# An attention and two feed-forward stages on one core: early memory for the first feed-forward unit, q stored twice, the sum of v on GpSimd, a written order for each of 18 tiles

## The chip, the cores and the metric

One Trainium2 chip, one of its cores. The metric is the device time of one execution in microseconds (us). The kernel before takes 2220.19 us, the median of 3 runs (2219.45 to 2221.54).

## The reference, cut to what matters

Three stages follow one another. The inputs are float32; `q`, `k` and `v` have the shape (4, 8, 576, 64).

```python
scores = (1 / 8) * q @ k.T                       # 32 heads, 576 x 576 each
scores = where(scores >= rowmax(scores) - tau, scores, -1e9)
attn = exp(scores - rowmax(scores)); attn /= attn.sum(-1) + 1e-9
x = merge_heads(attn @ v)                        # 2304 x 512
x = (((x @ w1) * (x @ w2)) @ w3) @ w_out         # first feed-forward stage
P = exp(x @ w_gate - max); 8 times: P /= rowsum; P /= colsum; P *= 2304 / 8
out = sum over 8 experts e of P[:, e] * (relu(x @ w1[e]) @ w2[e])
```

## The kernel before, in words

**Attention.** The 32 heads are taken as 16 pairs (`NP`). A pair has nine tiles: four blocks of 128 query rows for each of two heads, and a ninth that holds the last 64 rows of both. So there are 144 tiles (`NT`), and the loop at L322 runs over slots s = 0 to 153. In slot s the kernel does a step of several tiles at once: the scores of tile s+2 (step `S`, L142, TensorE), their row maximum (`x`, L146, VectorE), the threshold and the exponential (`t` L149, `X` L154, ScalarE), the mask of tile s (`m`, L161, VectorE), the four transposes of tile s-1 (`T`, L186, TensorE) and their copy out of PSUM (`e`, L191, ScalarE), and in some slots the product with v (`v`, L232), the transposed last columns of three tiles (`q` L197, `l` L202) and the spreading of the inverse sums (`I` L250, `V` L262, `o` L270). Scores have two PSUM buffers (L134), so the scores of tile s+2 can only be written when the mask of tile s has been read from the same buffer. Where tau is negative no score of a row is kept and the reference's row becomes uniform; the flags `g` and the sums `s` (L171 to L177, GpSimd) account for that, and it needs the column sum of v, which `vsum` (L204 to L210) makes with five matmuls of float32 in slot 1 of each pair (`SUMS_AT`).

**Filling.** Meanwhile `W34` (L357) takes 40 pieces of weights, which arrive as 64-bit bit patterns, converts them to float32 (`to_f32`, L478: per piece two ScalarE, four VectorE and two GpSimd operations) and forms w3 @ w_out in 192 matmuls of 128x512 (`w`, L460). `CONVERT` and `PRODUCTS` say by slot (modulo 18) how many steps of a conversion and how many matmuls are allowed; `CHUNKS` is the order of the pieces. `c` and `z` in the order each do at most one conversion step.

**Order.** Each engine runs its instructions in program order. Within a slot the order of the steps is written out as one string for all slots:

```python
ORDER = "fTmSvrigesIzVocxqlXwyt"
```

After the steps of a slot come the loads for the next pair (L341, L345), the sum of v (L343) and, from slot 142 on, steps of the feed-forward generator (`AHEAD`, L347).

**Start.** For the first pair q and k come by four transfers for each head (L106 to L111, both halves of 64 partitions apart: q goes to both, k's columns are split), then tau (L287), then the first weights (L289) and v. ScalarE negates tau (L291) before the thresholds and exponentials of the first two tiles.

**Feed-forward.** `Moe` (L502) splits each float32 operand in a high and a low part and does three products. Work is cut in units: 24 for the first stage (alternately `a` = w1 and `b` = w2 columns, for three blocks of 768 tokens), then 96 for the experts. A unit has seven slots of six matmuls (`mm1`, L663); while they run, the products of the unit before with the second weights (L741) are put between them, and the weights of the next unit are prepared by `prep1` (L571 to L598) on GpSimd and ScalarE. The first unit needs four sums of blocks of x (`xsum`, L629), seven splits (`xsplit`, L655: ScalarE L659, VectorE L660) and its weights. All that is allocated at slot 142, when the pool of q, k and the conversions is closed (L327); the loads of the second unit's weights start when `grow` (L533) is called in slot 145, where the pool of w3 @ w_out is closed.

Of the kernel before, what the change touches and what calls it, by code (L numbers as in the profile page):

```python
# [22 lines left out]
NP = B * H // 2  # L23
# [26 lines left out]
AFTER = {'I': (7, 10), 'V': (8, 11), 'o': (8, 11), 'y': (8, 12)}  # L50
SUMS_AT, VALUES_AT = 1, 4
# [22 lines left out]
def attention(k):  # L74

    tc, nc = k.tc, k.nc
    early, late, banks, parts34 = ExitStack(), ExitStack(), ExitStack(), ExitStack()
    pool = late.enter_context(tc.tile_pool(name="att", bufs=1, side="right"))
    psum = late.enter_context(tc.tile_pool(name="attp", bufs=1, space=bass.MemoryType.PSUM, side="right"))
    epool = early.enter_context(tc.tile_pool(name="atte", bufs=1))  # L80
    wpool = parts34.enter_context(tc.tile_pool(name="w34s", bufs=1, side="right"))
    psums = banks.enter_context(tc.tile_pool(name="atts", bufs=1, space=bass.MemoryType.PSUM))
# [206 lines left out]
    fill = W34(k, epool, wpool, psum)  # L289
# [31 lines left out]
    ahead = iter(())  # L321
    for s in range(NT + 10):  # L322
        n, t = divmod(s, 9)
        if s == NT - 20:
            k.raw0 = wpool.tile([128, 4, 256], F32, name="raw1_0")
            nc.sync.dma_start(k.raw0.rearrange("p a b -> p (a b)"), k.wab["a"][0])
# [20 lines left out]
        if k.moe:  # L347
            for _ in range(AHEAD.get(s - NT, 0)):
                next(ahead)
    late.close()  # L350
    k.moe.rest()
    for _ in ahead:
        pass
    k.moe.stack.close()
# [147 lines left out]
class Moe:  # L502
# [7 lines left out]
    def __init__(self, k):  # L510
# [7 lines left out]
        self.xh = [pool.tile([128, 2, HT], F32R, name=f"xh{i}") for i in range(7)]  # L518
        self.xl = [pool.tile([128, 2, HT], F32R, name=f"xl{i}") for i in range(7)]
# [6 lines left out]
        self.sink = []  # L526

# [14 lines left out]
    def rest(self):  # L542
# [5 lines left out]
        self.acc = self.pool2.tile([128, 6, DM], F32, name="acc")  # L548
        self.load2()
        self.load2()  # L550

# [311 lines left out]
    def run(self):  # L863
        units = self.units
        self.raw1[0] = self.k.raw0
# [144 lines left out]
```

## Time and profile before

| What | Before |
|---|---|
| median of 3 runs | 2220.19 us |
| the profiled execution, its time | 2223.54 us |
| the profiled execution, its span | 2221.6 us |
| PE (TensorE) busy | 2171.8 us, 98% of the span |
| DVE (VectorE) busy | 1229.4 us, 55% |
| ACT (ScalarE) busy | 947.1 us, 43% |
| POOL (GpSimd) busy | 990.9 us, 45% |
| scores of the last tile begin | 401.79 us |
| first matmul of the feed-forward stages begins | 419.04 us |

The span goes from the first to the last instruction of the profiled execution; 1.9 us of its time lie around it. The attention takes the first fifth of the span, the feed-forward stages the rest. Matmuls overlap one another, so the time that one costs is the distance from its start to the start of the next, not its own duration. In the timeline, "[idle before <-releaser]" names what the engine waited for.

### The profile page before, as it was taken

The numbers are of one execution on the slowest core, as the hardware profiler recorded it, in microseconds if no ns is written. First come the engines' busy times: TensorE is split into PE (matmuls) and PEld (weight loads), VectorE is DVE, ScalarE is ACT, GpSimd is POOL, SyncE is SP. The second block draws the span as 40 slices with busy tenths as digits, with TensorE's granted clock in tenths as the row PEclk, the third lists the DMA queues.
The fourth block names the chain that finished last, engine by engine and source line by source line (L and its number), as shares of the span: only waits on it lengthen the run. The fifth ranks groups of instructions, "written<-read, shape, count | busy, mean of one in ns | idle before, by whom it ended". The sixth has DMA issues, their size and how long they took to land.

```text
span 2221.6 us, 32300 instructions
## 1 busy us (share of the span) xinstructions
PE 2171.8 (98%) x12624; PEld 1894.7 (85%) x12624; DVE 1229.4 (55%) x2122; ACT 947.1 (43%) x1770; POOL 990.9 (45%) x970
## 2 busy tenths in 40 slices
PE   7899999899999999999999999999999999999999
PEld 4666666699999899999999999999999999999998
DVE  7888888765465555444445534444445434444444
ACT  6877877543233343333334343333334343333332
POOL 4545454670003444444456444444456444444441
PEclk9999999999999999999999999999999999999999
DMA  4343434367554121121212212121212212121121
GB/s 137 102 124 119 129 109 130 130 254 262 202 200 157 59 74 64 70 76 58 76 57 81 89 69 76 58 76 57 76 62 77 100 58 76 57 76 66 68 76 39
DMA packets 62809, 218.12 MB, mean 98 GB/s; under 512 B 7488, under 2 KB 11584, under 8 KB 62656
## 3 DMA queue, kind: packets, MB, share of 16 engines
q1 hardware_dynamic: 62656, 216.05, 28.3%
q8 instruction: 99, 1.62, 0.3%
q14 instruction: 54, 0.44, 0.1%
HBM read 185.61 MB, written 30.41 MB: 97 GB/s over the span
## 4 chain that ended last, share of the span: by engine, by line
PE 92%; DVE 6%; issue 1%; ACT 1%; DMA 1%; POOL 0%; SPq 0%; ACTq 0%; DVEq 0%; POOLq 0%
PE ye L741 40%; PE py L671 22%; PE px L671 16%; PE s L142 4%; PE pv L232 3%; PE t L186 2%; PE w L460 2%; DVE p L161 2%; DVE nmx L146 2%; PE vs L209 1%; PE tt L197 1%; PE py L820 0%; DVE x L281 0%; DVE cvq L495 0%; DVE c L726 0%
## 5 line engine op out<-in xcount | busy, mean ns | idle before, releaser
L741 PE MATMUL ye<-w2h,hl 128*128 128x512 f32 x1152 | 451.6, 392 | 0.0
L741 PE MATMUL ye<-w2h,hh 128*128 128x512 f32 x1152 | 451.3, 392 | 0.0
L741 PE MATMUL ye<-w2l,hh 128*128 128x512 f32 x1152 | 451.0, 391 | 0.0
L736 ACT ACTIVATE hh<-c 128x384 fp32r<-128x384 f32 x288 | 151.4, 526 | 604.9 <-DVE c L715 604.8
L598 POOL TENSOR_TENSOR w1l<-wt,w1h 128x1024 fp32r<-128x1024 f32 x104 | 253.2, 2435 | 287.6 <-ACT w1h L595 287.6
L671 PE MATMUL py<-xh,w1h 128*128 128x384 f32 x960 | 322.4, 336 | 2.2 <-DVE ca L711 1.4
L671 PE MATMUL py<-xh,w1l 128*128 128x384 f32 x960 | 322.7, 336 | 0.3 <-POOL w1l L598 0.3
L671 PE MATMUL py<-xl,w1h 128*128 128x384 f32 x960 | 322.5, 336 | 0.0
L593 POOL TENSOR_TENSOR w1l<-raw,w1h 128x256 fp32r<-128x256 f32 x104 | 79.9, 768 | 469.1 <-ACT w1h L587 469.1
L741 PEld LDWEIGHTS ye<-w2l,hh 128*128 128x128 f32 x1152 | 216.3, 188 | 32.9 <-DVE w2l L621 0.3
L741 PEld LDWEIGHTS ye<-w2h,hl 128*128 128x128 f32 x1152 | 216.2, 188 | 32.6
L671 PE MATMUL px<-xh,w1h 128*128 128x384 f32 x720 | 242.6, 337 | 0.7 <-ACT ca L709 0.4
L671 PE MATMUL px<-xl,w1h 128*128 128x384 f32 x720 | 242.1, 336 | 0.0
L671 PE MATMUL px<-xh,w1l 128*128 128x384 f32 x720 | 242.0, 336 | 0.0
L741 PEld LDWEIGHTS ye<-w2h,hh 128*128 128x128 f32 x1152 | 216.3, 188 | 24.6
L586 POOL TENSOR_TENSOR wt<-raw 128x512 f32<-128x512 f32 x104 | 138.8, 1335 | 199.5 <-DMA raw<-in_e 182.4
L671 PEld LDWEIGHTS py<-xh,w1h 128*128 128x128 f32 x960 | 180.7, 188 | 24.6 <-DVE c L715 3.5
L671 PEld LDWEIGHTS py<-xl,w1h 128*128 128x128 f32 x960 | 180.6, 188 | 17.3
L698 DVE TENSOR_TENSOR u<-py,p 128x384 f32<-128x384 f32 x120 | 66.7, 556 | 214.5 <-PE py L671 213.5
L671 PEld LDWEIGHTS py<-xh,w1l 128*128 128x128 f32 x960 | 180.4, 188 | 0.6 <-POOL w1l L598 0.6
L737 DVE SCALAR_TENSOR_TENSOR hl<-c,hh 128x384 fp32r<-128x384 f32 x288 | 166.9, 580 | 9.2
L736 ACT ACTIVATE hh<-px 128x384 fp32r<-128x384 f32 x96 | 47.2, 492 | 272.7 <-PE px L671 269.8
(141 smaller groups left out, 3901.2 us busy)
## 6 DMA issues: line engine op xcount, KB each, us to landing
raw<-in_e SPq DMA_DIRECT2D x192, 512.0 KB, 4.0
wraw<-in_w SPq DMA_DIRECT2D x32, 512.0 KB, 4.1
w1h<-w_kept SPq DMA_DIRECT2D x16, 896.0 KB, 5.0
w1l<-w_kept SPq DMA_DIRECT2D x16, 896.0 KB, 6.9
rq<-in_qk SPq DMA_DIRECT2D x30, 288.0 KB, 5.3
w_kept<-w1h SPq DMA_DIRECT2D x8, 896.0 KB, 7.7
w_kept<-w1l SPq DMA_DIRECT2D x8, 896.0 KB, 9.0
raw<-w SPq DMA_DIRECT2D x12, 512.0 KB, 3.6
```

Of the source, the lines that this page charges most:

```text
L142: nc.tensor.matmul(out[:, c, 0:KH], lhsT=q[rows, g, cols], rhs=kk[rows, g], start=True, stop=True)
L146: nc.vector.tensor_reduce(out=nmx[:, s % 18:s % 18 + 1], in_=ps[:, :, 0:288], axis=AX.XY, op=ALU.max, negate=True)
L161: nc.vector.scalar_tensor_tensor(out=ppool[g][:, i, 0:S].rearrange("p (a b) -> p a b", a=2), in0=ps[:, :, 0:288], scalar=thr[:, s % 18:s % ...
L232: nc.tensor.matmul(ps, lhsT=rv[:, h, i] if i < 4 else rv[0:65, h, 4], rhs=l[:, i] if i < 4 else tail, start=i == 0, stop=i == 4)
L586: nc.gpsimd.tensor_tensor(out=t[:, 0:2], in0=raw[:, 1:3], in1=raw[:, 0:2], op=ALU.subtract)
L593: nc.gpsimd.tensor_tensor(out=wl[:, 0], in0=raw[:, 0], in1=f32(wh[:, 0]), op=ALU.subtract)
L598: nc.gpsimd.tensor_tensor(out=wl[:, 3:7], in0=t, in1=f32(wh[:, 3:7]), op=ALU.subtract)
L671: self.nc.tensor.matmul(out, lhsT=w[:, wi, o], rhs=x[xi][:, d], start=n == 0 and not adds, stop=n == 5, skip_group_check=True)
L698: tt(out=self.u2, in0=py, in1=self.p1, op=ALU.add)
L736: nc.scalar.activation(hi, src, AF.Relu)
L737: self.later.append(lambda: nc.vector.scalar_tensor_tensor(out=lo, in0=src, scalar=0.0, in1=f32(hi), op0=ALU.max, op1=ALU.subtract))
L741: self.queue.append((out.shape[-1], lambda: self.nc.tensor.matmul(out, lhsT=l, rhs=r, start=start, stop=stop, skip_group_check=True)))
```

## The change

- The order of a slot becomes a table: `ORDER` has 18 strings, one for each slot modulo 18, and `CONVERT`, `PRODUCTS`, `CHUNKS`, `AFTER` and `AHEAD` have other values.
- q and k lie in the input so that both halves of 64 partitions come with one transfer: two transfers for each head of the first pair instead of four, two for each later pair instead of four. tau is loaded behind the first head, and the exponential of the first tile goes ahead of the negation of tau and the threshold.
- The five blocks of v are added by three operations on GpSimd (`presum`, in slot 5 of the pair before), and `vsum` has one matmul instead of five, in slot 4 instead of 1. v is loaded in slot 3 instead of 4.
- `Moe` is made at the start. Its sums of x and the weights of its first unit have memory from then on, and `AHEAD` starts at slot 128. The conversions get a pool of their own, which is closed when they are done and gives room for four of the seven splits (`room`); the pool of q and k gives room for the other three in slot 142. The splits 4 to 6 are made in slots 0 to 2 of the first unit.
- `rest` loads the second weights before it allocates the accumulator.

```diff
-CONVERT = (0, 0, 1, 1, 1, 2, 0, 1, 3, 2, 0, 1, 1, 1, 2, 2, 1, 1)
-PRODUCTS = (1, 0, 0, 0, 4, 1, 1, 0, 4, 1, 0, 0, 2, 4, 2, 3, 3, 4)
-ORDER = "fTmSvrigesIzVocxqlXwyt"
+CONVERT = (1, 2, 2, 0, 0, 3, 0, 0, 3, 0, 1, 3, 0, 2, 1, 1, 0, 1)
+PRODUCTS = (3, 4, 0, 0, 1, 2, 3, 0, 4, 0, 3, 0, 0, 1, 4, 0, 3, 1)
+ORDER = ('wsmTqSfVIviocylrezgxtX', 'msiTSzyVfcqgxwretIXvol', 'imsTSvofwcgIezxltrqyVX', 'TmszVreSviyocxIgfqtlXw', 'mTIVqySvorzseliwcfgxtX', 'msTwVfiSeocyIvgzxlqrtX', 'omTreVfzSqgxwvltXyIcis', 'wmTsSfxvryeiqlVzoIXctg', 'gmTSiVzreIvcofxqlwtsXy', 'miVogTqSvsIcwzyexfrtXl', 'gTmysiSrewfoVcqzxIXtvl', 'VolTsqymiSwcgzfxIvretX', 'mTfoSvcireyszVgxqwtIXl', 'lmszycVTIeoiwfvSgxrtqX', 'ymlTsqwcreVoSfvIzgxtXi', 'moTeSscqzgxyfwVlIvrtXi', 'ymzwoTigSvqxfcreIlsVXt', 'TmSrleIvVzosfcwgxitXqy')
-AHEAD = {-2: 1, -1: 2, 0: 1, 1: 1, 2: 3, 3: 1, 4: 1, 5: 1, 6: 1, 7: 1}
+AHEAD = {-16: 1, -15: 1, -14: 1, -13: 1, -12: 3, -11: 0, -10: 0, -9: 0, -8: 0, -7: 0, -6: 3, -5: 0, -4: 0, -3: 0, -2: 2, -1: 0, 0: 1, 1: 3, 2: 3, 3: 1, 4: 1, 5: 0, 6: 1, 7: 2}
-CHUNKS = "oowoooo33o3o33ww3ww3333wwww3w33w3ww3ww3w"
+CHUNKS = "owooooo3o3o333w3ww3w3w3w3w33ww33ww3ww3ww"
-AFTER = {'I': (7, 10), 'V': (8, 11), 'o': (8, 11), 'y': (8, 12)}
-SUMS_AT, VALUES_AT = 1, 4
+AFTER = {'I': (7, 10), 'V': (8, 11), 'o': (8, 12), 'y': (8, 13)}
+PRESUM_AT = 5
+SUMS_AT = 4
+VALUES_AT = 3
...
     def fetch(n, h):
-        for half in range(2):
-            rows = slice(64 * half, 64 * half + 64)
-            nc.sync.dma_start(raws["k", n][rows, h], k.qk[n, :, 2 + h.start:2 + h.stop, KH * half:KH * half + KH])
-        for half in range(2):
-            nc.sync.dma_start(raws["q", n][64 * half:64 * half + 64, h], k.qk[n, :, h])
+        nc.sync.dma_start(raws["k", n][:, h], k.qk[n, :, h, S:S + KH])
+        nc.sync.dma_start(raws["q", n][:, h], k.qk[n, :, h, 0:S])
...
+    def presum(n):
+        rv = raws["v", n]
+        add = lambda out, a, b: nc.gpsimd.tensor_tensor(out=out, in0=a, in1=b, op=ALU.add)
+        a = epool.tile([128, 2, 2, D], F32, tag="va", name=f"va{n}", bufs=1)
+        o = raws["s", n] = epool.tile([128, 2, D], F32, tag="vp", name=f"vp{n}", bufs=1)
+        add(a, rv[:, :, 0:2], rv[:, :, 2:4])
+        add(a[:, :, 0], a[:, :, 0], a[:, :, 1])
+        add(o, a[:, :, 0], rv[:, :, 4])
+
     def vsum(n):
...
-        for i in range(5):
-            nc.tensor.matmul(ps[0:65, 0:128], lhsT=last, rhs=rv[:, :, i], start=i == 0, stop=i == 4)
+        nc.tensor.matmul(ps[0:65, 0:128], lhsT=last, rhs=raws.pop(("s", n)), start=True, stop=True)
...
     load(0)
-    for h in range(2):
-        fetch(0, slice(h, h + 1))
+    fetch(0, slice(0, 1))
     nc.sync.dma_start(k.ntau, k.tau.to_broadcast([128, 1]))
+    fetch(0, slice(1, 2))
...
-    nc.scalar.mul(k.ntau, k.ntau, -1.0)
     load_v(0)
+    presum(0)
     scores(0)
     scores(1)
     for s in range(2):
         rowmax(s)
+        expo(s)
+        if s == 0:
+            nc.scalar.mul(k.ntau, k.ntau, -1.0)
         thresh(s)
-        expo(s)
...
-    ahead = iter(())
+    ahead = moe.run()
...
-        if s >= NT - 2 and k.moe is None and fill.gen is None:
+        if fill.gen is None and moe.rooms == 0:
+            conv.close()
+            moe.room(0, 4)
+        if s >= NT - 2 and moe.rooms == 1:
             early.close()
-            k.moe = Moe(k)
-            ahead = k.moe.run()
-        if s == NT:
-            banks.close()
-            k.moe.banks()
-        if s == NT + 1:
-            assert fill.done()
+            moe.room(4, 7)
+        if moe.rooms == 2 and moe.pool is None and fill.done():
             parts34.close()
-            k.moe.grow()
-        for what in ORDER:
+            moe.grow()
+        for what in ORDER[s % 18]:
...
+        if t == PRESUM_AT and n + 1 < NP:
+            presum(n + 1)
...
+        if s == NT - 1:
+            banks.close()
+            moe.banks()
+        for _ in range(AHEAD.get(s - NT, 0)):
+            next(ahead)
...
     def run(self):
         units = self.units
-        self.raw1[0] = self.k.raw0
         prep = self.prep1(0)
-        for slot in range(7):
-            if slot < 4:
-                self.xsum(0, slot, self.nc.vector)
-            self.xsplit(0, slot)
-            if slot >= 1:
-                next(prep, None)
+        for i in range(4):
+            self.xsum(0, i, self.nc.vector)
+            next(prep, None)
             yield
         for _ in prep:
-            pass
+            yield
+        for slot in range(4):
+            while not self.rooms:
+                yield
+            self.xsplit(0, slot)
+            yield
+        while self.xy is None or self.pool is None:
+            yield
...
-            splits, turns = {}, {}
+            splits, turns = {0: 4, 1: 5, 2: 6} if u == 0 else {}, {}
```

## Rows read from the trace of the kernel before

**Rows 1.** Busy time by engine in one stretch: us, then PE, PEld, DVE, ACT, POOL, PEclk, DMA.
```profile
500.00:560.00 60.00, 60.00 (x340) 56.76 (x339) 34.38 (x58) 18.30 (x31) 0.00 (x0) 1.00 0.66 245
```
**Rows 2.** The chain of waits over one attention slot: start us, us, what.
```profile
371.06 0.78 PE s L142 x4
...
371.87 0.76 DVE nmx L146
372.62 0.74 DVE p L161 x2
...
373.41 0.76 PE s L142 x4
```
**Rows 3.** The timeline of PE over two attention slots, and of one with the sum of v.
```profile
339.87 0.60 PE L186 MATMUL t<-ident,p 128*128 128x128 f32 x4
...
341.09 1.09 PE L232 MATMUL pv<-pt,rv 128*64 128x128 f32 x16
...
342.34 0.44 PE L262 MATMUL rb<-ident,rw 128*128 128x128 f32 x2
...
342.72 0.60 PE L186 MATMUL t<-ident,p 128*128 128x128 f32 x4
...
343.94 0.69 PE L232 MATMUL pv<-pt,rv 128*64 128x64 f32 x16
...
344.67 0.54 PE L197 MATMUL tt<-ident,p 128*65 128x128 f32 x3
344.97 0.48 PE L460 MATMUL w<-wol,w3h 128*128 128x512 f32 x1
345.28 0.39 PE L460 MATMUL w<-woh,w3l 128*128 128x512 f32 x1
345.51 0.60 PE L186 MATMUL t<-ident,p 128*128 128x128 f32 x4
...
363.66 1.31 PE L209 MATMUL vs<-rv,last 128*65 128x128 f32 x10
364.80 0.60 PE L186 MATMUL t<-ident,p 128*128 128x128 f32 x4
```
**Rows 4.** The four VectorE steps of a conversion, each by its line: ns min/median/max.
```profile
L489 DVE TENSOR_SCALAR cva<-wraw x40: 396/421/1081, 11.3 to 387.6; 128x512 int32<-128x512 int32 x40
L492 DVE SCALAR_TENSOR_TENSOR cva<-wraw,cva x40: 685/690/1649, 14.5 to 389.8; 128x512 int32<-128x512 int32 x40
L495 DVE SCALAR_TENSOR_TENSOR cvq<-cvq,cva x40: 679/693/1793, 15.3 to 392.8; 128x512 f32<-128x512 f32 x40
L497 DVE TENSOR_SCALAR cvs<-cvq x40: 391/399/1059, 17.5 to 395.8; 128x512 int32<-128x512 int32 x40
```
**Rows 5.** The start: timeline (SP, PE) and, in the middle, the chain of waits.
```profile
0.72 1.21 SPq L109 DMA_DIRECT2D rk<-in_qk  x2
...
5.81 3.50 DMA ntau<-in_tau
...
11.69 1.33 PE L142 MATMUL s<-ks,rq 64*128 64x288 f32 x4 [3.99 <-DVE cva L489]
```
**Rows 6.** Sums of x by their line (ns min/median/max), and the page's DMA issues of v.
```profile
L633 DVE TENSOR_TENSOR s<-x x8: 927/949/1000, 404.1 to 665.3; 128x768 f32<-128x768 f32 x8
...
rv<-in_vv SPq DMA_DIRECT2D x16, 320.0 KB, 3.0
```
**Rows 7.** From attention to feed-forward: timelines of PE and POOL, the third from the chain.
```profile
401.79 0.72 PE L142 MATMUL s<-ks,rq 64*64 64x288 f32 x8
...
409.05 1.09 PE L186 MATMUL t<-ident,p 128*128 128x128 f32 x4 [2.44 <-DVE p L161]
...
419.40 4.84 DMA raw<-w_b
...
424.40 1.28 POOL L586 TENSOR_TENSOR wt<-raw 128x512 f32<-128x512 f32 x1 [3.06 <-DMA raw<-w_b]
...
431.67 0.44 PE L671 MATMUL py<-xh,w1l 128*128 128x384 f32 x1 [0.30 <-POOL w1l L598]
```

More of the change, by code (lines that the diff above doesn't have):

```diff
@@ L76, in attention @@
     tc, nc = k.tc, k.nc
-    early, late, banks, parts34 = ExitStack(), ExitStack(), ExitStack(), ExitStack()
+    early, late, banks, parts34, conv = (ExitStack() for _ in range(5))
+    moe = Moe(k)
     pool = late.enter_context(tc.tile_pool(name="att", bufs=1, side="right"))
     psum = late.enter_context(tc.tile_pool(name="attp", bufs=1, space=bass.MemoryType.PSUM, side="right"))
-    epool = early.enter_context(tc.tile_pool(name="atte", bufs=1))
+    cpool = conv.enter_context(tc.tile_pool(name="attc", bufs=1))
     wpool = parts34.enter_context(tc.tile_pool(name="w34s", bufs=1, side="right"))
+    epool = early.enter_context(tc.tile_pool(name="atte", bufs=1, side="right"))
     psums = banks.enter_context(tc.tile_pool(name="atts", bufs=1, space=bass.MemoryType.PSUM))
@@ L284, in attention @@
     load(0)
-    for h in range(2):
-        fetch(0, slice(h, h + 1))
+    fetch(0, slice(0, 1))
     nc.sync.dma_start(k.ntau, k.tau.to_broadcast([128, 1]))
+    fetch(0, slice(1, 2))
     nc.scalar.activation(thr[:, 0:1], k.ident[:, 0:1], AF.Exp)
-    fill = W34(k, epool, wpool, psum)
+    fill = W34(k, cpool, wpool, psum)
     prep(0, slice(0, 1))
-    nc.scalar.mul(k.ntau, k.ntau, -1.0)
     load_v(0)
+    presum(0)
     scores(0)
@@ L324, in attention @@
         if s == NT - 20:
-            k.raw0 = wpool.tile([128, 4, 256], F32, name="raw1_0")
-            nc.sync.dma_start(k.raw0.rearrange("p a b -> p (a b)"), k.wab["a"][0])
-        if s >= NT - 2 and k.moe is None and fill.gen is None:
-            early.close()
-            k.moe = Moe(k)
-            ahead = k.moe.run()
-        if s == NT:
-            banks.close()
-            k.moe.banks()
-        if s == NT + 1:
-            assert fill.done()
+            moe.raw1[0] = wpool.tile([128, 4, 256], F32, name="raw1_0")
+            nc.sync.dma_start(moe.raw1[0].rearrange("p a b -> p (a b)"), k.wab["a"][0])
+        if fill.gen is None and moe.rooms == 0:
+            conv.close()
+            moe.room(0, 4)
+        if s >= NT - 2 and moe.rooms == 1:
+            early.close()
+            moe.room(4, 7)
+        if moe.rooms == 2 and moe.pool is None and fill.done():
             parts34.close()
-            k.moe.grow()
-        for what in ORDER:
+            moe.grow()
+        for what in ORDER[s % 18]:
             if what in steps:
@@ L344, in attention @@
             vsum((s - SUMS_AT) // 9)
+        if t == PRESUM_AT and n + 1 < NP:
+            presum(n + 1)
         if n < NP and t == VALUES_AT:
             load_v(n + 1)
-        if k.moe:
-            for _ in range(AHEAD.get(s - NT, 0)):
-                next(ahead)
+        if s == NT - 1:
[3 more added lines that the diff above has]
+            next(ahead)
+    assert moe.pool and moe.xy
     late.close()
-    k.moe.rest()
+    moe.rest()
     for _ in ahead:
         pass
-    k.moe.stack.close()
+    moe.stack.close()
 class W34:
@@ L517, in __init__ @@
         self.pool = self.odd = self.pool2 = None
-        self.xh = [pool.tile([128, 2, HT], F32R, name=f"xh{i}") for i in range(7)]
-        self.xl = [pool.tile([128, 2, HT], F32R, name=f"xl{i}") for i in range(7)]
+        self.xh, self.xl, self.xy, self.rooms = [None] * 7, [None] * 7, None, 0
         self.xs = [pool.tile([128, 2, HT], F32, name=f"s{i}") for i in range(4)]
@@ L526, in __init__, with room @@
         self.sink = []
+    def room(self, a, b):
+        pool = self.stack.enter_context(self.k.tc.tile_pool(name=f"moex{a}", bufs=1))
+        self.rooms += 1
+        for i in (self.SLOTS[slot][0] for slot in range(a, b)):
+            self.xh[i] = pool.tile([128, 2, HT], F32R, name=f"xh{i}")
+            self.xl[i] = pool.tile([128, 2, HT], F32R, name=f"xl{i}")
     def banks(self):
@@ L547, in rest @@
         self.yb = [psum.tile([128, 512], F32, name=f"ye{i}") for i in range(6)]
-        self.acc = self.pool2.tile([128, 6, DM], F32, name="acc")
         self.load2()
         self.load2()
+        self.acc = self.pool2.tile([128, 6, DM], F32, name="acc")
     def kept(self, u):
@@ L964 @@
     k.wk = dram.tile([8, 2, 128, 7 * 256], F32, name="w_kept")
-    k.moe = None
     attention(k)
@@ L973, in _layouts @@
     q = pairs(inputs["q"])
-    qk = c(np.concatenate([a.transpose(0, 3, 1, 2) for a in (q, pairs(inputs["k"]))], axis=2))
+    q, kk = (a.transpose(0, 3, 1, 2) for a in (q, pairs(inputs["k"])))
+    qk = np.concatenate([np.concatenate([q, kk[..., KH * i:KH * i + KH]], axis=3) for i in range(2)], axis=1)
     v = pairs(inputs["v"])
@@ L987, in _layouts @@
     return dict(
-        qk=qk, vv=vv, tau=inputs["tau"].reshape(1, 1),
+        qk=c(qk), vv=vv, tau=inputs["tau"].reshape(1, 1),
         w1=bits(first(inputs["moe_w1"])[0]), w2=bits(first(inputs["moe_w2"])[0]),
```

## The prediction

> **What bounds the kernel now.** I first ask where TensorE is already full. From 500 us on it is: 60.00 of 60 us busy at a granted clock of 1.00 [rows 1]. The change leaves the feed-forward work as it is, so that block only moves forward or back. What can change lies before about 445 us: the start, the 144 tiles of attention, and the passage to the first units.
>
> In the attention two things compete in each slot. One is a loop between two engines: scores (0.78), their maximum on VectorE (0.76), the mask (0.74), and then the next scores into the buffer that the mask has read. A slot that does nothing else lasts 373.41 - 371.06 = 2.35 us [rows 2]. The other is TensorE's own list. Start to start, transposes and scores take 341.09 - 339.87 = 1.22, a product with v 1.25, the spreading 0.38, the last product of a pair 0.73, three tail transposes 0.30, a filling matmul 0.31 behind another operation and 0.23 behind its like, the sum of v 1.14 [rows 3]. The two slots shown there last 2.85 and 2.79: TensorE's list sets them, while a slot with no product with v falls back to the loop. So time is lost because the list is uneven: full slots run at the list, thin ones wait for the loop.
>
> I add this up for each of the 141 slots between the scores of tile 2 (11.69 [rows 5]) and of the last tile (401.79 [rows 7]), with the lists that the tables of the code give. TensorE's lists sum to 350 us, the loop (with the conversion steps that don't fit into the 0.8 us in which VectorE waits for scores, at the medians of rows 4) to 351 us, and the larger of the two, slot by slot, to 382. The trace has 401.79 - 11.69 = 390.1; the first 18 slots, at half clock (1.33 us for scores at 11.69 [rows 5] against 0.76 [rows 2]), make up most of the rest. The rule describes the kernel.
>
> **The middle, part by part.** Eight of the ten records of each sum of v go: 1.14 becomes 0.25, 16 times, so 14 us of TensorE's lists; eight filling matmuls also come after the last scores instead of before (2 us). The lists sum to 334. The loop doesn't get shorter: 347. What the 18 orders do is even out the lists: filling matmuls no longer stand in slots with a product with v, where T, S and v alone are 2.47, but in the thin ones, some ahead of the scores, where TensorE waits for the mask. Slot by slot the larger of the two sums to 356, 26 less. Conversions are sometimes held, up to 1.65 or 1.79 us instead of 0.69 [rows 4]; with a quarter on each step the sums are 389 before and 367 after, 22 less. The loop now binds more slots than the list, so I take 22.
>
> Against that stands what moves into these slots. The four sums of x now lie on VectorE behind the maximum of slots 128 to 131: 4 x 0.95 = 3.8 us at their median [rows 6], and all on the loop there; the first unit's weight pieces run beside them on GpSimd and can hold them, so I count 5. The sum of v on GpSimd is 256, 128 and 128 elements; GpSimd takes 1.28 us for 512 [rows 7], so 1.3 to 1.7 us per pair, 27 at most in all. GpSimd has room (45% busy). What it can do is hold a VectorE conversion: below by nothing, above by 0.75 (its longest operation) for each of 16 pairs, 12 us. Most conversions are at their minimum already though GpSimd does two operations for each of them [rows 4], so I take 2. Middle: 22 - 5 - 2 = 15 us, ends 26 - 4 = 22 and 6.
>
> How the rule of the Trainium skill stands to this (SBUF — State Buffer, section "SBUF: two separate sides"): VectorE operations with two SBUF inputs and GpSimd operations share a port pair that one holds for a whole instruction. It speaks against the move; by it every sum of v that meets a conversion would hold it, and the middle would give 5 us rather than 15. The longest conversions in rows 4 agree with such holding, the medians say that it is the exception.
>
> **The start.** SP issues a transfer each 0.6 us [rows 5]. Eight stand before tau, whose landing at 5.81 + 3.50 = 9.31 lets ScalarE go on to the first threshold and exponential. After the change two stand before it: it lands some 3.6 us earlier, and the first exponential no longer waits for it at all. The first scores then start about 0.9 us earlier (two issues fewer, each for twice the partitions), the exponential and threshold follow at once, and the mask of tile 0, the keys of the second head and the scores of tile 2 come at about 9.1 instead of 11.69: 2.6 us, ends 1 and 4. SP has the first weights 2.6 us earlier too. Later pairs issue two transfers less; SP is far from full, which I cost at nothing. The sum of v of pair 0 waits on GpSimd for v (3.0 us to land [rows 6]) and is done at about 10, before the flags of slot 1 are due behind it.
>
> **The passage.** From the last tile's scores (401.79) to the second slot of the second unit (431.67) are 29.9 us [rows 7], of which TensorE's own list at full clock is about 17.5 (16.3 to that unit's first slot). It waits 2.44 for the last mask, which stands behind a split on VectorE, and then runs at half clock (1.09 us for four transposes [rows 7] against 0.60 [rows 3]); at the end it waits for the second unit's weights: their load is issued at 419.40, lands 4.84 later, and GpSimd works on the pieces from 424.40 until the matmul at 431.67 can go on. That load waited for GpSimd to finish the first unit's weights, because it takes their memory.
>
> After the change the sums of x and those pieces are done by slot 132. Not so the splits: counted from the tables, the last conversion ends in slot 141, so both rooms open in slot 142, and the steps that `AHEAD` grants in slots 132 and 138 find no room and do nothing but finish the weights. The splits begin where they began before; two still stand on VectorE ahead of the last mask, which I let wait another 1 us for. But the load of the second unit's weights now waits only for the end of the filling (its last matmuls are two slots later, in slot 143, about 6.5 us after the last scores; the copy, its store and the issue bring 8 to 10), lands at 13 to 15 and is prepared at 20 to 22. TensorE's list, with the eight matmuls that moved here, is 18.2 plus 1.2 of the unit's first slot and 1 to 2 of waiting. So that slot starts at about 22 to 23 instead of 29.9: 7 us, ends 2 and 10. In the units behind it the preparation still runs beside VectorE's work as now; nothing for that. The order of allocation in `rest` touches only addresses: zero, and if a load waited longer for them the products with it, several us later, would cover that.
>
> **Sum.** 2.6 + 15 + 7 = 24.6 us. Against the profiled execution (2223.54, span 2221.6) that is 2198.9; its time is 3.35 above the median of the runs, and for the median I forecast 2220.2 - 24.6 = 2195.6 us. Changes of less than 0.2% (4.4 us) can't be told from none.
>
> **The rivals.**
> *The port takes the middle back.* Each sum of v and each piece of the first unit's weights holds a VectorE operation on the loop: another 10 us, 2206. For it: the loop binds more slots, and the longest rows 4. Against: the medians.
> *All of it comes.* The middle gives 22, the passage 10: 2220.2 - 34.6 = 2186. For it: the rule fits the slots before within a tenth of a us mostly. Against: two bounds this close seldom leave no wait.
> *The first unit is not early at all.* The splits begin in slot 142 as before; if the weights' load also stays where it was, the passage gives nothing: 2203.
> *Slower: the sum of v delays the spreading.* It stands on GpSimd ahead of the sums, inverse copies and through them the spreading on TensorE (slot 8). If v landed later than the two slots (about 5 us) between its load and the sum, GpSimd would stand; one slot of delay in each of 15 pairs is 15 x 2.5 = 37 us, 2233. It decides only if v takes over some 7 us; it lands in 3.0 [rows 6], and its load waits for one product of slot 3 at most.
>
> **How the numbers follow.** Forecast, 2188 to 2203: 0.55. Port: 0.20. All of it: 0.12. Not early: 0.04. Near no change, by several mishaps of size: 0.05. Slower: 0.04. So faster 0.90, the same 0.06, slower 0.04. The range 2184 to 2209 leaves out the far ends of the second and third and all that is slower.
>
> **What would show it.** After: 32 records of the sum of v instead of 160; 18 slots in 46 to 47 us instead of 49; the scores' waits for the mask no fewer than now, as the loop binds; tau landed before 6 us and the scores of tile 2 near 9; the load of the second unit's weights 8 to 10 us after the last scores; the first product with second weights some 24 us earlier. Conversions with means far over 0.7 us, or sums of x of 2 us, would show the port; TensorE idle before the spreading, the slower rival; an unchanged distance from the last scores to the second unit, the fourth.

## The result, and the profile after

The changed kernel takes 2193.11 us, the median of 4 runs (2192.25 to 2196.12), beside 2220.02 for the kernel before in the same comparison: a ratio of 0.9878, interval 0.9866 to 0.989. Compared again later it gave 2192.03 and 0.9871 (0.9856 to 0.9886). The forecast was 2195.6, in a range of 2184 to 2209.

Three marks divide the trace as the forecast did: the scores of tile 2, the scores of the last tile, and the second slot of the second unit.

| us | before | after | gained | forecast |
|---|---|---|---|---|
| scores of tile 2 begin | 11.69 | 8.71 | 2.98 | 2.6 |
| from there to the scores of the last tile, 141 slots | 390.10 | 370.36 | 19.74 | 15 |
| from there to the second slot of the second unit | 29.88 | 22.89 | 6.99 | 7 |
| from there to the end of the span | 1789.9 | 1788.5 | 1.4 | 0 |

The trace gives 31.1 us, the medians 26.9. The profiled execution of before was 3.35 above the median shown with it, as the forecast said; the one of after (2192.25) lies 0.9 below its own. From the last mark on, every run of this study had 1787.9 to 1789.9 us left, so the feed-forward block only moves.

The page's busy times of after, first: GpSimd has 36.4 us more than before, VectorE 8.5 less.

```profile
PE 2153.5 (98%) x12496; PEld 1873.0 (86%) x12496; DVE 1220.9 (56%) x2122; ACT 948.0 (43%) x1770; POOL 1027.3 (47%) x1018
```

**The start**, in the timeline of after (start us, us, engine, line, operation; in brackets the idle time before it and its releaser), answers to [rows 5].

```profile
0.72 0.39 SPq L111 DMA_DIRECT2D rk<-in_qk  x1
...
1.64 0.42 SPq L295 DMA_DIRECT2D ntau<-in_tau  x1
...
6.36 0.74 ACT L155 ACTIVATE e<-s,nmx 128x576 f32<-128x576 f32 x1 [2.90 <-DVE nmx L147]
...
7.00 0.19 ACT L308 ACTIVATE ntau<-ntau 128x1 f32<-128x1 f32 x1
...
8.71 1.33 PE L143 MATMUL s<-ks,rq 64*128 64x288 f32 x4 [2.22 <-ACT ks L126]
```

tau is issued at 1.64 instead of 5.81 and lands 3.2 us later, at 4.9. ScalarE no longer waits for it: its first exponential is released by the maximum, and tau's negation finds it in memory.

**The middle.** The waits of TensorE from 37 us to the last scores (who, waited for whom: us in all, times, longest):

```profile
PE s L143 <- DVE p L162: 11.9, 24, 1.5
...
PE rb L271 <- POOL rw L259: 0.7, 1, 0.7
```

Before, the same view (40 to 404 us) had 19.2 us in 34 waits of the scores for the mask. A slot that does little still lasts the loop's 2.35 us [rows 2], but matmuls now fill most of that time. Eighteen slots last 46.3 to 46.6 us instead of 48.8 to 49.9, save the first eighteen (48.57, before 52.11) and the last fifteen of the 141 (42.81, before 41.89).

The sum of v, in the groups by line of after from 37 us on (shapes, count | busy us, mean ns | idle before), is three GpSimd operations and one matmul, which has two records. [Rows 3] have the five of before.

```profile
L207 POOL TENSOR_TENSOR va<-rv 128x256 f32<-128x256 f32 x14 | 13.9, 990 | 1.8 <-DMA rv<-in_vv 1.8
...
L207 POOL TENSOR_TENSOR va<-va 128x128 f32<-128x128 f32 x14 | 7.5, 538 | 1.1
L207 POOL TENSOR_TENSOR vp<-va,rv 128x128 f32<-128x128 f32 x14 | 6.7, 478 | 1.1
L218 PE MATMUL vs<-vp,last 128*65 128x128 f32 x30 | 6.2, 288 | 0.0
```

Those 14 pairs cost GpSimd 28.1 us, 2.0 each, more than the 1.3 to 1.7 forecast.

**Where it lost.** A slot is timed from the scores of the slot ahead of it to its own scores. Slots 129 to 132 last 4.44, 3.30, 3.22 and 3.81 us; before they lasted 2.85, 2.88, 2.35 and 3.49. VectorE's timeline in the first of them shows the first sum of x between a maximum and the mask, as the forecast put it:

```profile
343.16 0.75 DVE L147 TENSOR_REDUCE nmx<-s 128x1 f32<-128x576 f32 x1
343.83 0.95 DVE L654 TENSOR_TENSOR s<-x 128x768 f32<-128x768 f32 x1
344.69 0.81 DVE L162 SCALAR_TENSOR_TENSOR p<-s,thr,e 128x576 f32<-128x576 f32 x1
```

**The passage** answers to [rows 7]: the timeline of after, TensorE, SP and GpSimd.

```profile
379.07 0.72 PE L143 MATMUL s<-ks,rq 64*64 64x288 f32 x8
...
386.64 0.63 PE L187 MATMUL t<-ident,p 128*128 128x128 f32 x4 [1.13 <-DVE p L162]
...
401.96 0.33 PE L692 MATMUL py<-xh,w1l 128*128 128x384 f32 x1
...
388.68 0.43 SPq L589 DMA_DIRECT2D raw<-w_b  x1
...
392.51 1.29 POOL L607 TENSOR_TENSOR wt<-raw 128x512 f32<-128x512 f32 x1 [0.99 <-DMA raw<-w_b]
...
398.68 2.40 POOL L619 TENSOR_TENSOR w1l<-wt,w1h 128x1024 fp32r<-128x1024 f32 x1
```

The load of the second unit's weights goes out 9.6 us after the last scores (17.6 before), GpSimd begins on it at 13.4 and ends at 22.0, and the matmul that was late in [rows 7] starts at 22.9 without a wait. The transposes behind the last mask wait 1.13 us instead of 2.44 and run at full clock (0.63 us for four).

Before, TensorE had a longer wait still, which [rows 7] do not show and the forecast did not count, for the last inverse copies (timeline of before):

```profile
417.81 0.44 PE L262 MATMUL rb<-ident,rw 128*128 128x128 f32 x2 [3.34 <-POOL rw L250]
```

GpSimd could not copy earlier: VectorE began the inverse at 416.49, behind three sums of x and three splits that stood after the last mask. With the sums gone from there, the same wait is 0.24 us.

### The profile page after: what moved, and what is told of

The parts are those of the page before. It is cut to its first block, busy times and chain, and to the rows that moved or that the text cites. A ratio compares the mean times of both kernels' runs of the same rounds, so it can differ in the third digit from the quotient of the medians.

```text
span 2190.5 us, 31914 instructions
## 1 busy us (share of the span) xinstructions
PE 2153.5 (98%) x12496; PEld 1873.0 (86%) x12496; DVE 1220.9 (56%) x2122; ACT 948.0 (43%) x1770; POOL 1027.3 (47%) x1018
## 4 chain that ended last, share of the span: by engine, by line
PE 89%; DVE 6%; ACT 2%; issue 2%; POOL 0%; DMA 0%; SPq 0%; ACTq 0%; POOLq 0%; DVEq 0%
PE ye L762 40%; PE py L692 22%; PE px L692 17%; PE s L143 4%; PE pv L241 2%; PE t L187 2%; DVE p L162 2%; DVE nmx L147 1%; PE w L474 1%; DVE cva L506 1%; PE tt L198 0%; ACT e L155 0%; PE py L841 0%; PE rb L271 0%; DVE c L747 0%
```

## The experiments

My theory after the result: the gain is made by the orders and tables together with the move of the sum of v; the sums of x cost what the forecast said; and the early first unit returns in the passage about what it takes in slots 129 to 132. "141 slots" and "passage" below are the second and third rows of the table above; after has 370.36 and 22.89.

**1. The sum of v back on TensorE**

```diff
-        nc.tensor.matmul(ps[0:65, 0:128], lhsT=last, rhs=raws.pop(("s", n)), start=True, stop=True)
+        for i in range(5):
+            nc.tensor.matmul(ps[0:65, 0:128], lhsT=last, rhs=rv[:, :, i], start=i == 0, stop=i == 4)
...
-    presum(0)
...
-        if t == PRESUM_AT and n + 1 < NP:
-            presum(n + 1)
```

> The changed kernel with the sum of v back on TensorE: five matmuls in slot 4, the three GpSimd operations gone. Theory of lists and loop (each slot lasts as long as the larger of TensorE's list and the loop scores, maximum, mask): 16 sums of 0.9 us more make 14 us of lists, but only 9.5 us by the slot-by-slot rule (356 to 365), and 1 to 2 come back where VectorE's inverse no longer waits for GpSimd; the 141 slots take 377 to 380 us instead of 370.4, the time is 2200 to 2203. Rival, TensorE's work alone counts: 14 us, 2207. Rival, the port: the sum of v on GpSimd holds 0.75 us of VectorE per pair, so taking it away gives back as much as it costs: the 141 slots at 366 to 371, 2189 to 2194.

2201.13 us, ratio 0.9913 (0.9898 to 0.9927): 8.0 us over the changed kernel. The 141 slots take 378.07, 7.7 more. The passage, which has no sum of v in it, is also longer, 25.52. Its timeline, TensorE:

```profile
408.33 0.41 PE L690 MATMUL py<-xh,w1h 128*128 128x384 f32 x1 [1.57 <-DVE ca L730]
...
410.09 0.52 PE L690 MATMUL px<-xh,w1h 128*128 128x384 f32 x1
410.41 0.52 PE L690 MATMUL px<-xl,w1h 128*128 128x384 f32 x1
```

After the wait of 1.57 us matmuls start 0.32 us apart instead of 0.17, until 412.0: the granted clock is 0.50 between 409 and 412. That loss is hardly in the median: the profiled execution is the longest of the four (2202.70 us at a mean granted clock of 0.999; the others 2200.51 to 2201.55 at 1.00). So the move of the sum of v is worth about 8 us, nearly all of them in the slots. This run also prices what it does to VectorE. The four conversion steps from 37 us on, in the groups by line, of after:

```profile
L506 DVE SCALAR_TENSOR_TENSOR cva<-wraw,cva 128x512 int32<-128x512 int32 x36 | 37.0, 1026 | 0.5
L509 DVE SCALAR_TENSOR_TENSOR cvq<-cvq,cva 128x512 f32<-128x512 f32 x37 | 25.3, 684 | 0.8
L503 DVE TENSOR_SCALAR cva<-wraw 128x512 int32<-128x512 int32 x36 | 22.7, 631 | 0.0
L511 DVE TENSOR_SCALAR cvs<-cvq 128x512 int32<-128x512 int32 x37 | 15.6, 421 | 0.0
```

They sum to 100.6 us; without GpSimd's sums of v the same rows have 32.9, 28.1, 22.3 and 15.6, together 98.9. One step grew by 4.1 us with the sums of v and another shrank by 2.8, so 1.7 us is the net of conversions that were held and others that were held less.

**2. One order for all slots, with the new tables**

```diff
-ORDER = ('wsmTqSfVIviocylrezgxtX', 'msiTSzyVfcqgxwretIXvol',
...
+ORDER = ("fTmSvrigesIzVocxqlXwyt",) * 18
```

> The changed kernel with the one order of before for all 18 slots; its tables for conversions, products and pieces stay. Theory of lists and loop: by the slot-by-slot rule 387 instead of 356 us, so the 141 slots take 395 to 402 us instead of 370.4 and the whole gain of the middle is gone, though TensorE has 14 us less to do; 2218 to 2226. Rival, the shorter sum of v made the middle faster and the orders add little: the 141 slots at 370 to 378, 2193 to 2201.

2225.43 us, ratio 1.0023 (1.0014 to 1.0032), slower than before. The 141 slots take 404.27, 33.9 us more than with the 18 orders, the other marks do not move (8.73 and 22.91). One slot in TensorE's timeline, and its longest group of waits from 37 us on:

```profile
261.33 0.76 PE L143 MATMUL s<-ks,rq 64*128 64x288 f32 x4 [0.76 <-DVE p L162]
...
262.01 1.09 PE L241 MATMUL pv<-pt,rv 128*64 128x128 f32 x16
...
263.56 0.47 PE L474 MATMUL w<-woh,w3l 128*128 128x512 f32 x1
...
264.86 0.76 PE L143 MATMUL s<-ks,rq 64*128 64x288 f32 x4
```

```profile
PE s L143 <- DVE p L162: 33.4, 49, 3.2
```

The slot from 261.33 holds a product with v, tails and three filling matmuls one after another and lasts 3.53 us by TensorE's list alone. Of 88 slots in the middle of this run sixteen last 3.25 to 3.55 us; the longest of after there lasts 3.05. The thin slots still wait: 33.4 us for the mask where after has 11.9. The work is the same, and an uneven list costs both ways.

**3. The old tables, with the 18 orders**

```diff
-CONVERT = (1, 2, 2, 0, 0, 3, 0, 0, 3, 0, 1, 3, 0, 2, 1, 1, 0, 1)
-PRODUCTS = (3, 4, 0, 0, 1, 2, 3, 0, 4, 0, 3, 0, 0, 1, 4, 0, 3, 1)
+CONVERT = (0, 0, 1, 1, 1, 2, 0, 1, 3, 2, 0, 1, 1, 1, 2, 2, 1, 1)
+PRODUCTS = (1, 0, 0, 0, 4, 1, 1, 0, 4, 1, 0, 0, 2, 4, 2, 3, 3, 4)
...
-CHUNKS = "owooooo3o3o333w3ww3w3w3w3w33ww33ww3ww3ww"
+CHUNKS = "oowoooo33o3o33ww3ww3333wwww3w33w3ww3ww3w"
```

> The changed kernel with the conversions, products and pieces tables of before and the 18 orders kept. Theory of lists and loop: 379 instead of 356 us by the slot-by-slot rule, and the 10 to 15 us by which the changed kernel lies over the rule: the 141 slots at 388 to 396, 2211 to 2220; orders and tables only work together. Rival, the orders carry the gain of the middle by themselves: 370 to 376, 2193 to 2199.

2265.09 us, ratio 1.0204 (1.0188 to 1.0219), with 141 slots in 441.26: far over what either theory gave. TensorE's longest group of waits from 37 us on; one of its eleven in the timeline of GpSimd and TensorE; and the window from 40 to 380 us (us, then PE, PEld, DVE, ACT, POOL busy, granted clock, DMA):

```profile
PE rb L271 <- POOL rw L259: 30.6, 11, 3.6
```

```profile
317.24 1.28 POOL L512 TENSOR_TENSOR cvl<-cvl,cvs 128x512 f32<-128x512 f32 x1
...
318.59 1.26 POOL L513 TENSOR_TENSOR wf<-cvl,cvq 128x512 f32<-128x512 f32 x1
...
319.80 0.86 POOL L259 COPY rw<-rin 128x256 f32<-128x256 f32 x1
...
320.71 0.69 PE L271 MATMUL rb<-ident,rw 128*128 128x128 f32 x2 [3.56 <-POOL rw L259]
```

```profile
40.00:380.00 340.00, 285.37 (x2461) 193.56 (x2461) 252.27 (x505) 239.23 (x521) 182.15 (x287) 0.94 0.33 106
```

The spreading waits 30.6 us for an inverse copy on GpSimd, a wait that after has for 0.7. This is the mechanism of the slower rival, there for another cause: the two conversion operations of that slot stand on GpSimd ahead of the copy. And the granted clock falls to 0.94 in the mean, where after and the kernel before have 1.00 in the same window. If that mean is of 1.00 and 0.50, 41 of the 340 us ran at half, which costs some 20 us: an estimate. The other waits grew too, those for the mask to 25.4 us; all of TensorE's waits in that view sum to 66 us, where after has 16.

**4. The first unit late again**

```diff
-AHEAD = {-16: 1, -15: 1, -14: 1, -13: 1, -12: 3, -11: 0, -10: 0, -9: 0, -8: 0, -7: 0, -6: 3, -5: 0, -4: 0, -3: 0, -2: 2, -1: 0, 0: 1, 1: 3, 2: 3, 3: 1, 4: 1, 5: 0, 6: 1, 7: 2}
+AHEAD = {-2: 2, -1: 2, 0: 3, 1: 3, 2: 3, 3: 1, 4: 1, 5: 1, 6: 1, 7: 2}
```

> The changed kernel with the sums of x and the first unit's weights back behind the last scores (from slot 142 on) and nothing of the generator in slots 128 to 132. Theory: the passage (last scores to the second slot of the second unit) was shortened because the load of the second unit's weights no longer waits for GpSimd to finish the first unit's: it goes back from 22.9 to 28 to 32 us, while slots 129 to 132 lose their 4.6 us of waiting, so the 141 slots take 365 to 366 us instead of 370.4; together 2193 to 2199. Rival, the passage was shortened by what the order puts there (filling matmuls in slots 142 and 143) and not by the weights: it stays at 23 to 25 us, 2188 to 2190.

2193.16 us, ratio 0.9875 (0.9859 to 0.9892): no difference from the changed kernel that could be told. The parts are different, though. The 141 slots take 365.32, 5.0 less, and slots 129 to 132 10.07 instead of 14.77. The passage takes 29.10, 6.2 more, about the 29.9 of before. TensorE in the timeline of this run:

```profile
373.95 0.72 PE L143 MATMUL s<-ks,rq 64*64 64x288 f32 x8
...
385.35 0.45 PE L692 MATMUL px<-xh,w1h 128*128 128x384 f32 x1 [2.95 <-ACT xh L680]
...
388.10 0.69 PE L692 MATMUL px<-xl,w1h 128*128 128x384 f32 x1 [2.30 <-DVE xl L681]
...
403.05 0.33 PE L692 MATMUL py<-xh,w1l 128*128 128x384 f32 x1
```

TensorE waits 2.95 and 2.30 us for splits, and goes on at half clock (at 388.59 and 388.91 two matmuls of 0.52 start 0.32 apart; at full clock 0.17). So the early unit is what shortens the passage, and it pays for that in the slots. The reason that I gave for it, the load of the second unit's weights, is not what binds here. The load goes out 12.3 us after the last scores (9.6 in after), and GpSimd ends its work on these weights at 26.3, 2.8 us before TensorE comes to them at 29.1 without a wait:

```profile
397.85 2.42 POOL L619 TENSOR_TENSOR w1l<-wt,w1h 128x1024 fp32r<-128x1024 f32 x1 [0.71 <-ACT w1h L616]
```

**5. q and k by halves of 64 partitions**

```diff
-        nc.sync.dma_start(raws["k", n][:, h], k.qk[n, :, h, S:S + KH])
-        nc.sync.dma_start(raws["q", n][:, h], k.qk[n, :, h, 0:S])
+        for half in range(2):
+            rows = slice(64 * half, 64 * half + 64)
+            nc.sync.dma_start(raws["k", n][rows, h], k.qk[n, rows, h, S:S + KH])
+        for half in range(2):
+            rows = slice(64 * half, 64 * half + 64)
+            nc.sync.dma_start(raws["q", n][rows, h], k.qk[n, rows, h, 0:S])
```

> The changed kernel with q and k again by two transfers of 64 partitions each (same input, same bytes), tau still behind the first head and behind the first exponential. Theory: of the 3.0 us that the start gained, the transfers' issue made about 1: the scores of tile 2 begin at 9.5 to 10.2 us instead of 8.7, everything later is shifted by that; SP's two more issues per pair cost nothing; 2194 to 2195. Rival, the start was tau's wait alone: scores of tile 2 at 8.7 to 8.9, no change. Rival, SP's issue counts in the later pairs too: 15 x 1 us or more, 2208.

2194.05 us, ratio 0.9881 (0.9866 to 0.9896). The issues of SP at the start, in its timeline ("x2" is two transfers):

```profile
0.72 1.20 SPq L113 DMA_DIRECT2D rk<-in_qk  x2
...
3.24 0.59 SPq L299 DMA_DIRECT2D ntau<-in_tau  x1
```

The scores of tile 2 begin at 9.96 instead of 8.71. So 1.25 of the start's 2.98 us are the transfers; 1.7 are left, by difference, for tau and the exponential. The whole is not worth a measurable time by itself.

**6. The sum of v three slots later**

```diff
-PRESUM_AT = 5
+PRESUM_AT = 8
```

> The changed kernel with the sum of v on GpSimd at the end of slot 8 of the pair before instead of slot 5. Theory: what it costs the loop is small wherever it stands (in slot 16 of 18 VectorE's inverse waits 0.45 us for the sums queued behind it, which goes; some conversion near slot 8 may be held): the 141 slots at 369 to 371.5, 2192 to 2195. Rival, its place is what makes it harmless: elsewhere it holds conversions or the inverse on the loop, 0.5 to 1 us per pair, 378 to 386 and over 2200.

2204.24 us, ratio 0.9933 (0.9917 to 0.995): 12 us over the changed kernel beside it (2192.03), where the move had brought 8. The 141 slots take 381.72. TensorE's waits for the mask and for the inverse copies there, its timeline and GpSimd's in the slots that suffer, and a window among them:

```profile
PE s L143 <- DVE p L162: 15.3, 22, 1.6
PE rb L271 <- POOL rw L259: 5.8, 6, 1.7
```

```profile
276.10 0.76 PE L143 MATMUL s<-ks,rq 64*128 64x288 f32 x4 [1.02 <-DVE p L162]
...
278.61 0.69 PE L271 MATMUL rb<-ident,rw 128*128 128x128 f32 x2 [0.85 <-POOL rw L259]
...
280.29 1.33 PE L143 MATMUL s<-ks,rq 64*128 64x288 f32 x4
...
273.18 0.92 POOL L207 TENSOR_TENSOR va<-rv 128x256 f32<-128x256 f32 x1
...
278.16 0.40 POOL L259 COPY rw<-rin 128x256 f32<-128x256 f32 x1
```

```profile
279.00:282.00 3.00, 3.00 (x15) 1.92 (x15) 0.83 (x3) 1.84 (x4) 2.67 (x3) 0.50 0.46 179
```

GpSimd works in program order: the sum of v goes ahead of the flags and the inverse copies, these come late, TensorE waits 5.8 us for the copies where after has 0.7, and behind a wait of 1.02 and one of 0.85 it works at a granted clock of 0.50 (scores in 1.33 us instead of 0.76). The queue is not all of it. The four conversion rows here are 35.9, 31.8, 22.6 and 15.6, together 105.9 us, 5.3 more than with the sum in slot 5, and the scores' wait for the mask is 15.3 where after has 11.9. So in slot 8 the sum of v also holds conversions that the loop waits for, as the port rival had it. How the 12 us divide between the queue, the held conversions and the clock, no run separates. The slower rival had a price of this kind in mind, and v's landing as its cause; the place alone is enough.

**7. The sums of x on GpSimd, spread out**

```diff
+SUM_SLOTS = (92, 101, 110, 119)
...
+        if s in SUM_SLOTS:
+            moe.xsum(0, SUM_SLOTS.index(s), nc.gpsimd)
...
-            self.xsum(0, i, self.nc.vector)
```

> The changed kernel with the four sums of x on GpSimd, one each at the end of slots 92, 101, 110 and 119, and no longer on VectorE in slots 128 to 131. Theory: there they lay on the loop and cost the 4.6 to 5 us by which the early first unit pays for its shorter passage; on GpSimd, which is half idle, they lie beside it. Slots 129 to 132 go from 14.8 to 10.1 to 11 us, the 141 slots from 370.4 to 365.5 to 367, the passage stays at 23: 2187.5 to 2190. Rival, the port: each sum holds VectorE's conversions on the loop for its 1.9 us and delays what GpSimd owes the loop: 2 to 4 us come back in slots 92 to 121, 2191 to 2193.

2191.35 us, ratio 0.9868 (0.9853 to 0.9882), too near the 2192.03 of the changed kernel in its second comparison to tell. Slots 129 to 132 fall from 14.77 to 11.73 us, but slot 93 is 1.07 longer and slot 112 0.81; the slots behind the other two sums lose nothing. Both engines in slot 93:

```profile
247.26 1.81 POOL L657 TENSOR_TENSOR s<-x 128x768 f32<-128x768 f32 x1
...
247.82 1.80 DVE L509 SCALAR_TENSOR_TENSOR cva<-wraw,cva 128x512 int32<-128x512 int32 x1
```

A conversion step that takes 0.69 alone [rows 4] takes 1.80 beside a GpSimd operation of 1.81, and ends 0.55 us after it. The Trainium skill (SBUF — State Buffer, "SBUF: two separate sides") has these two engines share a port pair that one of them holds for a whole instruction; this row agrees with it.

**8 and 9. The keys of the next pair one slot earlier.** Slots 25, 43, 97 and 115 (slot 7 of 18) last 2.73 us where 61 and 79 last 2.33, behind a copy on ScalarE. Two runs move the copy that scales the keys, the second also to the end of its slot.

```diff
-LOAD_AT, KEYS_AT = 1, 5
+LOAD_AT, KEYS_AT = 1, 4
```

> The changed kernel with the scaling of the next pair's keys in slot 4 instead of 5. Theory: in slot 5 of 18 ScalarE has the copy, a conversion's two operations, a split and the keys (3.6 us against a slot of 2.35), so the copy of the transposes comes late and slot 7 lasts 2.74 instead of 2.33; without the keys there this goes: TensorE's waits of transposes for that copy fall from 3.8 to under 2 us, the 141 slots from 370.4 to 367 to 368.5, 2190 to 2192. Rival, ScalarE is not what slot 7 waits for: no change, 2193.

2193.2 us, ratio 0.9878 (0.9863 to 0.9893). Slot 97 falls from 2.74 to 2.33 us, slot 95 grows from 2.34 to 2.93: the wait only moved.

```diff
-LOAD_AT, KEYS_AT = 1, 5
+LOAD_AT, KEYS_AT = 1, 4
...
-  'mTIVqySvorzseliwcfgxtX'
+  'mTIVqySvozseliwcfgxtXr'
...
-  'lmszycVTIeoiwfvSgxrtqX'
+  'lmszycVTIeoiwfvSgxtqXr'
```

> The changed kernel with the keys scaled in slot 4 as the last ScalarE step there (in the earlier run they stood ahead of the copy of the transposes, slot 7 fell by 0.41 and slot 5 rose by 0.59). Theory: the 0.59 was the copy behind the keys; now slot 7 keeps 2.33 and slot 5 stays at 2.34: the 141 slots at 367 to 368, 2189.5 to 2191. Rival, ScalarE is as full in slot 4 and 5 wherever the keys stand: 370, 2192 to 2193.

2191.95 us, ratio 0.9873 (0.9859 to 0.9888), 141 slots in 370.00. Slot 97 stays at 2.71, so a later place for the keys does not relieve it. That does not clear the keys: here and in after ScalarE works almost without a gap for two slots up to the copy that slot 97 waits for (from 254.75 us here, from 255.00 in after), and the keys are part of that list in both.

**10 and 11. Better versions.** The first takes run 7 with sums where slots have fewer conversions, and the keys of run 9.

```diff
+SUM_SLOTS = (83, 101, 119, 137)
...
+        if s in SUM_SLOTS:
+            moe.xsum(0, SUM_SLOTS.index(s), nc.gpsimd)
```

> The changed kernel with two edits together: the sums of x on GpSimd at the end of slots 83, 101, 119 and 137 (in the run before with sums on GpSimd those after slots 101 and 119 cost the next slot nothing, those after 92 and 110 cost 1.07 and 0.81), and the keys scaled in slot 4 as the last thing ScalarE does there. Theory: 1.9 us of held conversions go against the earlier run with sums on GpSimd, and slot 7 of 18 loses its 0.4 without slot 5 gaining 0.6: the 141 slots at 364 to 366 (370 in the changed kernel), 2186 to 2189. Rival, each edit only moves a wait to another slot, as the keys before an earlier copy did: 369 and 2191 to 2193.

2189.06 us, ratio 0.9859 (0.9842 to 0.9875), the fastest of the study: its runs (2188.49 to 2189.27) lie below all runs of the changed kernel (2191.63 and more), though the intervals of the ratios overlap. The 141 slots take 367.37, slots 129 to 132 11.77, the passage 23.06. The new slots for the sums were not run without the new place of the keys, which brought nothing by itself (run 9).

The second has the sums in slots 83, 101, 105 and 119 and also spreads the first unit's weight pieces over slots 129 to 142:

```diff
-AHEAD = {-16: 1, -15: 1, -14: 1, -13: 1, -12: 3, -11: 0, -10: 0, -9: 0, -8: 0, -7: 0, -6: 3, -5: 0, -4: 0, -3: 0, -2: 2, -1: 0, 0: 1, 1: 3, 2: 3, 3: 1, 4: 1, 5: 0, 6: 1, 7: 2}
+AHEAD = {-15: 1, -12: 1, -7: 1, -4: 1, -3: 1, -2: 2, 0: 1, 1: 3, 2: 3, 3: 1, 4: 1, 6: 1, 7: 2}
```

> The changed kernel with the sums of x on GpSimd at the end of slots 83, 101, 105 and 119, and the five steps of the first unit's weights at the end of slots 129, 132, 137, 140 and 141: slots behind which VectorE has no conversion, or which cost nothing in the run with sums and keys. Theory, what is left of the cost of the early first unit is conversions held by GpSimd beside them: slots 129 to 132 take 10.1 to 10.5 us (11.8 with the steps in 128 to 132, 14.8 in the changed kernel), the 141 slots 365 to 366.5, the passage 23 to 24; 2186.5 to 2189. Rival, the steps hold VectorE or the spreading wherever they stand, or the last step delays the passage: 367 to 369 or a passage of 25, 2189 to 2192.

2190.53 us, ratio 0.9867 (0.985 to 0.9883). Slots 129 to 132 are down to 10.36, what they take in run 4 without the early unit (10.07), and the 141 slots to 365.87. But the passage takes 24.55, with these waits of TensorE in it:

```profile
380.83 0.44 PE L272 MATMUL rb<-ident,rw 128*128 128x128 f32 x2 [0.84 <-POOL rw L260]
...
396.74 0.41 PE L695 MATMUL py<-xh,w1h 128*128 128x384 f32 x1 [1.58 <-DVE ca L735]
```

TensorE's granted clock stayed at 1.00 behind both waits. What the slots gained, the end gave back in part. The pieces of the last slots stand on GpSimd ahead of the last inverse copies, which fits the first of these waits; no run separates it.

**12. The changed kernel once more**, without an edit, beside runs 6 to 8.

> The changed kernel as it is, beside the next three on the same chip: 2192 to 2195, the 141 slots 370 us.

2192.03 us (2191.63 to 2192.43), 141 slots in 369.90, passage 22.89: what differs by a us between runs is not a finding.

## Why the prediction was right

**The sum and its parts.** The forecast said 24.6, the medians say 26.9, and two of the three terms came within half a us: the start 2.98 for 2.6 and the passage 6.99 for 7. In the passage the load's distance (9.6 for "8 to 10 us"), its preparation (ended at 22.0 for "20 to 22") and the second slot (22.9 for "22 to 23") are as forecast, and run 4 shows that the early unit makes the difference: with the unit late again, 6.2 of the 7.0 us are gone.

**The right size of the passage is in part luck.** The forecast put it down first of all to the load of the second unit's weights. Before, TensorE's wait for them was 0.30 us [rows 7], and in run 4 it is nothing. What held TensorE was the work of the first unit on VectorE and ScalarE: before, 2.44 us for the mask behind a split and 3.34 for the last inverse copies; in run 4, 2.95 and 2.30 for splits; half clock behind them in both. The forecast has the 2.44 and the half clock and leaves out the 3.34. The two limits lie close together (in run 4 the weights are ready at 26.3 and TensorE comes to them at 29.1) and the early unit moved both, so counting the one gave the size of the other.

**The term that was mis-sized** is the middle: "22 - 5 - 2 = 15" measured 19.7. The 5 for the sums of x is right: run 4 has 5.0. Add it back, and the orders, tables and the sum of v brought 24.7, close to the 26 by the slot rule with conversions at their medians. Not all of that need be the orders': from 20 to 30 and from 30 to 40 us the granted clock was 0.82 and 0.84 in the profiled execution of before and 1.00 in after, by these means some 3.4 us, an estimate. That execution was also 3.35 us above its median, and the traces do not say in which part; by the medians the whole forecast was 2.3 short. As far as the traces go, what failed is the step to 22, "with a quarter on each step", and the 2 for the port. The quarter is there in VectorE's busy time: before, the four steps sum to 35.1 + 30.3 + 20.5 + 17.2 = 103.1 us, 2.8 a conversion, where the medians of [rows 4] give 2.2. So is the port's 1.7, a net (run 1). But I charged both to the loop. Part of that falls in slots where TensorE's list is the longer: in run 7 a sum of x on GpSimd cost 1.07 and 0.81 us in two places, and nothing in two others.

**The rival that the port takes the middle back** falls by run 1: moving the sum of v to GpSimd gains 8 us, and holds conversions by a net 1.7. Its mechanism is real (1.80 us in run 7's row), and its size hangs on the place: with the sum in slot 8 the same rows have 5.3 us more, and the slots lose more than the move gained (run 6). In slot 5 it was small, which the forecast took from the medians of [rows 4] and did not derive from the place. *All of it comes* was nearest beside the forecast: the middle came to 24.7 of its 26 before the sums of x. *Not early at all* falls by the passage.

**The slower rival** did not come: the spreading waits 0.7 us in all. Runs 3 and 6 show that this hangs on the order and on the place. With the sum of v in slot 8, or with the old tables, the spreading waits 5.8 or 30.6 us. I priced the mechanism and gave v's landing as the only thing that decides it; GpSimd's own queue decides it as well. The sum of v itself was priced low: 2.0 us a pair for "1.3 to 1.7", so some 32 for the "27 at most in all".

**A wrong sign.** I wrote "the scores' waits for the mask no fewer than now, as the loop binds". They fell from 19.2 us to 11.9. By the slot rule the loop does bind more slots. I take it that the filling matmuls that the 18 orders place ahead of the scores take up that time, as the trace puts a wait down only where TensorE has nothing to do; no run separates this. The other signs held: 32 records of the sum of v, 18 slots in 46.3 to 46.6, tau landed at 4.9, scores of tile 2 at 8.71, and the first product with second weights (409.85, before 439.65) came 29.8 us earlier where I said some 24, by the same misfit of the middle.

**The net of the early first unit.** The forecast's own sums said it: 7 in the passage, 5 of the sums of x against it. Run 4 measures 6.2 and 5.0 in the trace and nothing in the time. As built, that part of the change is worth about nothing; with the sums off VectorE (run 10) it is worth some 4 us by the medians of two comparisons, whose intervals overlap.

**What stays open.** Why slot 7 of 18 is 0.4 us late: the two runs moved the keys within ScalarE's list, and none took work out of it. How the losses in runs 3 and 6 divide between waits and the clock: no run separates them.

## What to carry to other kernels

Where two engines pass work in a loop and a third list runs beside it, sum per slot the larger of the two, with durations at their medians; that gave 26 us here where the trace shows 24.7 (some of it perhaps the clock's), and charging every held operation to the path made the estimate worse. The rule leaves out every other queue: for run 3, where GpSimd's queue was in the way, it gave 388 to 396 us and the slots took 441. An order of steps is tuned only together with its tables: either half alone (runs 2 and 3) was slower than the kernel before. Work moved to a less busy engine still stands in that engine's queue, so choose its slot by what is queued behind it and by what runs beside it: three slots made 12 us here, more than the move gained.

## What the runs showed of the hardware that I had not expected

At the start the issue of a transfer of 128 partitions of q or k took SP 0.39 to 0.43 us, and that of one of 64 partitions about 0.6 (1.20 and 1.23 for two, run 5), so there one for two halves saves more than half of the issue time. The partitions alone do not set that price: tau's own transfer, the same in all kernels, took 0.42 us in after and 0.59 in run 5, and the transfers of 128 partitions for the later pairs 0.55 us and more in after. What sets it, no run shows.

Short waits of TensorE can cost more than themselves: behind waits of 1.57 us (run 1), 2.95 and 2.30 (run 4), or 1.02 and 0.85 close together (run 6), matmuls went on at a granted clock of 0.50, for some 3 us in runs 1 and 6 and some 6 us in run 4. The length of a wait does not decide it. Waits of 1.58 us at the same place as run 1's (run 11, at 396.74) and of 2.33 us (run 2, at 379.55) were followed by a granted clock of 1.00, as was the wait of 1.13 in the passage of after.
